# Fourier mixing and a token MLP on one core: both DFTs from a quarter of their matrices, with the symmetry compared on the chip

## The chip, the cores and the metric

The kernel runs on one core of a Trainium2 chip. A core has TensorE (PE) for matmuls, VectorE (DVE), ScalarE (ACT) and GpSimd (POOL) for elementwise work, SyncE (SP) which here issues most loads, and 16 DMA engines between DRAM and the core's memory (SBUF). Matmuls write into eight banks of PSUM. The engines run their own instruction streams in order and wait for each other through semaphores. The metric is the device time of one execution in microseconds; the time before is the median of three runs.

## The reference

One array `x` of 2048 rows (tokens) and 640 columns (channels) goes through a layer norm, and three terms are added:

```python
xn = _layernorm(x, axis=-1)
a = jnp.einsum("bsd,ed->bse", xn, dft_hid_re)
b = jnp.einsum("bsd,ed->bse", xn, dft_hid_im)
y = einsum("ts,bse->bte", dft_seq_re, a) - einsum("ts,bse->bte", dft_seq_im, b)
h = _layernorm(xn, axis=-1)
u = _gelu(jnp.einsum("bsd,sf->bdf", h, w1) + b1)
m = (jnp.einsum("bdf,fs->bds", u, w2) + b2).transpose(0, 2, 1)
return x + y + m
```

The DFT matrices are inputs like any other: two of 2048 x 2048 for the sequence and two of 640 x 640 for the hidden axis, cosines and sines, all float32. `w1` is 2048 x 1728 and `w2` 1728 x 2048; the host lays both out with the last half block repeated, as 14 blocks of 128.

## The kernel before, in words

Every float32 product is made of three passes of a faster matmul format, in `three` (L158): each operand is split into a high part, written by ACT (`high`, L149), and a low part, the rest, written by DVE (`low`, L152). A pass each for high times high, high times low and low times high goes into the same bank. So each matrix piece that comes from DRAM costs an ACT and a DVE instruction before PE can use it; `cut_piece` (L182) makes the two.

The work is a list of `steps`; a step cuts one piece and runs its products. `turn_of(i)` (L1236) writes out the instruction order by hand for step i: its loads, reads of finished banks and sums, then the high part of step i+2 (`AHEAD = 2`), extra work, waiting `jobs`, the low part of step i+2, and last the products of step i. Three tiles take turns for the cut pieces.

The stages run one after the other:

- `first_columns` (L505 and on) computes the first of four column blocks of the sequence DFT directly while rows of `x` still come in and are normalized. Its order is the string `START`.
- `columns` (L599 and on) does the other blocks with a seven-product scheme: of a 2 x 2 block product, seven products instead of eight, with sums of operands made by DVE. Each step is one 128 x 512 piece of the sequence matrices. Results go through `store_y` (L499) to DRAM, partly by accumulating DMA issued on GpSimd.
- `hidden` (L1048 and on) reads them back and multiplies by the hidden matrices, again with seven products, and `collect` (L1044) adds the result to `out` by an accumulating DMA. `out` was first filled with `x` by a copy inside DRAM.
- `up` (twice) and `down` (twice) are the MLP, 49 and 56 steps each, in `row_steps`, with seven products too. Their 128 x 512 or 128 x 384 weight pieces are loaded on SP four to six steps ahead into eight slots (`raw_slot`). Rows of `x` are loaded and normalized again for the MLP by `rows_again`, with the combined factors of the two layer norms from `factors_again`; `moving_of` makes their seven operands in six jobs.

Of the kernel before, what the change touches and what calls it, by code (L numbers as in the profile page):

```python
# [10 lines left out]
BF16 = mybir.dt.bfloat16  # L11
AF = mybir.ActivationFunctionType
ALU = mybir.AluOpType

P = 128
S = 2048
# [17 lines left out]
BLOCK = 10  # L34
APART = 2
FIRST_STEP = 6
LAST_ROWS = (3, 6, 7)


FIRST = [  # L40
    (0, 0, 0, 5), (1, 0, 0, 3), (0, 1, 0, 5), (1, 1, 0, 3), (0, 4, 0, 5), (0, 5, 0, 5), (1, 4, 0, 5), (1, 5, 0, 5),
    (1, 0, 3, 5), (1, 1, 3, 5),
]

FIRST_AT = [0, 6, 1, 7, 2, 3, 4, 5, 6, 7]

START = """
    x0 W0 b0 b1 x1 b2 x4 b3 x5 b4 x2 x3 b5 x6 x7 b6 b7  # L50
    M0 A0 R0 T0-0 T0-1 E0 D0-0-2 D0-2-5 T1 y0 B0 z0 n0 L0 B1 T2 M1 A1 E1 R1 O1 D1-0-2 H1-2-5 y1 B2 z1 P0-0 P0-1 P1-0 P0-2 P1-1 P1-2 M4-0 n1 L1-0-2 L1-2-5 M4-1
    A4 E4 T3 T4 R4 B3 O4 V4 H4 M5 A5 E5 R5 N4 O5 V5 B4 P2
    L4 P3 H5 T5 M2 A2 N5 M3 A3 R2-3 B5 F2-3 L5 q4 P4
    H2 T6 N2 M6 A6 B6 L2 q5 P5 T7 M7 B7 A7
"""

def jobs_at(ahead, behind=(), light=()):
    return tuple({i: at.count(i) for i in at} for at in (ahead, behind, light))  # L60


JOBS_AT = (
    jobs_at((0, 1, 2, 4, 10, 12, 13, 14, 15, 16, 17, 18, 23, 25, 27), (2, 4, 10, 15, 16, 16, 17, 17)),
    jobs_at((0, 1, 2, 3, 4, 10, 12, 13, 14, 15, 18, 19, 20, 21, 22, 23, 26, 27), (0, 1, 2, 3)),
    jobs_at((0, 1, 2, 3, 4, 5, 41), (0, 1, 2, 3)),
    jobs_at((0, 1, 2, 3, 4, 13, 18, 19, 22, 27), (), (10, 14, 21)),
)
# [3 lines left out]
    (tuple(i for i in range(56) if i % 7 in (0, 1, 3, 6) and i != 6), 56), ((0, 1, 3, 4), 7),  # L72
# [5 lines left out]
def fnet_plus_mixer(  # L78
# [20 lines left out]

# [20 lines left out]
    idea = keep.tile([P, 1], F32, name="idea")  # L120

    mv = keep.tile([P, NS, 2], F32, name="mv")
    norm = keep.tile([P, 2, NS], F32, name="norm")
    again = keep.tile([P, 2, NS], F32, name="again")
    near = keep.tile([P, 2, NS], F32, name="near")
# [5 lines left out]
    x_slab = [  # L131
        keep.tile([P, 7, D], F32, name="x0", tag="slab4"), keep.tile([P, 1, D], F32, name="x1", tag="slab5"),
    ]
    x_in = [x_slab[k // 7][:, k % 7, :] for k in range(8)]
    nc.gpsimd.memset(x_in[0][:, H2 : H2 + P], 0.0)
    nc.scalar.dma_start(x_in[0][:, H2:], x_rows[0][:, H2:])
    part_up = [dram.tile([P, 2, D], F32, name=f"up{r}") for r in range(NF2)]
    y_part = [[dram.tile([P, ND, CH], F32, name=f"y{m}{c}") for c in range(NC)] for m in range(2)]


    nc.gpsimd.memset(eps, EPS)
    nc.gpsimd.tensor_scalar(idea, eps, EPS, eps, op0=ALU.add, op1=ALU.mult)
# [23 lines left out]
    bank_turn = [3]  # L166
# [4 lines left out]

# [6 lines left out]

    def cut_piece(source, n, tail=False, stacked=False):  # L182


# [7 lines left out]
        def top(part=None):  # L192
            if part:
                hi = held["piece"][:, 0, : n // 2]
                high(hi, source()[:, : n // 2])
                nc.tensor.matmul(psum[7][: P // 4, : P // 4], hi[:, : P // 4], hi[:, : P // 4], start=True, stop=True)  # L196
                return
            cut_turn[0] = (cut_turn[0] + 1) % (AHEAD + 1)
            held["piece"] = keep.tile([P, 2, D], R32, name="piece", tag=f"cut{cut_turn[0]}")
            if tail:  # L200
                hi, _, src = of_tail()
                high(hi, src)
            elif part is None:
                high(held["piece"][:, 0, :n], source())
            else:
                nc.vector.tensor_copy(held["piece"][:, 0, n // 2 : n], source()[:, n // 2 :])
# [15 lines left out]


    stats = {}

    def statistics(k, row, *halves):
        if k not in stats:
            stats[k] = small.tile([P, 2, 6], F32, name="st")
        for i in halves or range(2):
            nc.vector.bn_stats(stats[k][:, i, :], row[:, i * H2 : (i + 1) * H2])  # L230

    def aggregate(k):
        nc.vector.bn_aggr(mv[:, k, :], stats[k].rearrange("p a b -> p (a b)"))

    def root(var, q=None):

        if q is None:
            q = small.tile([P, NS], F32, name="q")[:, : var.shape[-1]]
        nc.scalar.activation(q, var, AF.Abs_reciprocal_sqrt, bias=eps)
        return var, q  # L240
# [8 lines left out]
    def offset_beside(to, k):  # L249
        nc.gpsimd.tensor_scalar(to[:, 1, k : k + 1], mv[:, k, 0:1], to[:, 0, k : k + 1], -1.0, op0=ALU.mult, op1=ALU.mult)  # L250

    halves_of = {}

    def half_beside(k, engine=nc.gpsimd):
        halves_of[k] = small.tile([P, 1], F32, name="half")
        engine.tensor_scalar(halves_of[k], mv[:, k, 1:2], EPS, -0.5, op0=ALU.add, op1=ALU.mult)

    squares_of = {}

    def squares_beside(k, engine):  # L260
        r, q = small.tile([P, 1], F32, name="beside"), near[:, 0, k : k + 1]
        squares_of[k] = r
        engine.tensor_scalar(r, halves_of[k], q, q, op0=ALU.mult, op1=ALU.mult)

    def refined(k, engine):
        q = near[:, 0, k : k + 1]
        engine.tensor_scalar(norm[:, 0, k : k + 1], squares_of[k], 1.5, q, op0=ALU.add, op1=ALU.mult)

    def factors_beside(k):
        squares_beside(k, nc.gpsimd)  # L270
        refined(k, nc.gpsimd)
        offset_beside(norm, k)

    def offset(to, ks):
        nc.vector.scalar_tensor_tensor(to[:, 1, ks], mv[:, ks, 0], -1.0, to[:, 0, ks], op0=ALU.mult, op1=ALU.mult)

    def factors(ks):
        inverse(norm[:, 0, ks], *root(mv[:, ks, 1]))
        offset(norm, ks)

    def factors_again():

        f = []

        def rooted():
            var = small.tile([P, NS], F32, name="var2")
            nc.vector.tensor_mul(var, mv[:, :, 1], norm[:, 0, :])
            nc.vector.tensor_mul(var, var, norm[:, 0, :])
            f.append(root(var))

        def inverted():
            inverse(again[:, 0, :], *f[0])
            nc.vector.tensor_mul(again[:, 0, :], again[:, 0, :], norm[:, 0, :])
            offset(again, slice(0, NS))

        return [rooted, inverted]

    def normalize(k, row, by, to=None):
        nc.scalar.activation(
            row if to is None else to, row, AF.Identity, scale=by[:, 0, k : k + 1], bias=by[:, 1, k : k + 1]  # L300
        )
# [19 lines left out]

    Q = 256
    slot = {1: 0, 2: 1, 4: 2, 5: 3, 6: 4, 3: 5, 7: 6}
    at_slot = {0: 0, 6: Q, 1: D, 2: D + Q, 3: 2 * D, 4: 2 * D + Q, 5: 2 * D + 2 * Q}
    at_fifth = (2 * Q, D + 2 * Q)
    fixed = [[None] * 4 for _ in range(2)]

    def part(a, which, i, n=1):
        return a[:, which, at_slot[i] : at_slot[i] + n * Q]

    def fifth(a, which, i):
        return a[:, which, at_fifth[i] : at_fifth[i] + P]

    def place_fixed(h, q):
        fixed[h][q] = keep.tile([P, 2, 8 * Q], R32, name=f"n{h}{q}", tag=f"slab{4 * h + q}")

    def sums_of_rows(h, q, row, lower, apart=False):  # L340


        def a(of, i):
            return of()[:, i * Q : (i + 1) * Q]

        def hi(i, src):
            high(part(fixed[h][q], 0, i), src)

        def lo(i, src):
            low(part(fixed[h][q], 1, i), src, part(fixed[h][q], 0, i))  # L350

        def job1():
            nc.vector.tensor_add(a(lower, 1), a(row, 1), a(lower, 1))
            hi(3, a(lower, 1))

        def job2():
            lo(3, a(lower, 1))
            sub(a(lower, 1), a(lower, 1), a(row, 0))
            hi(4, a(lower, 1))

        def job3():
            lo(4, a(lower, 1))
            sub(a(lower, 0), a(lower, 0), a(lower, 1))
            hi(5, a(lower, 0))

        def job4():
            lo(5, a(lower, 0))
            sub(a(row, 1), a(row, 0), a(row, 1))
            if not apart:
                job5()  # L370

        def job5():
            hi(6, a(row, 1))

        def job6():
            lo(6, a(row, 1))

        return [job1, job2, job3, job4] + [job5] * apart + [job6]


    for q in range(4):
        place_fixed(0, q)

    def first_rows(k, which, *ends):

# [3 lines left out]
        if APART <= k < 4:  # L389
            ends = (0, 2, 4, 5)  # L390
# [925 lines left out]
```

## Time and profile before

| what | us |
|---|---|
| median of 3 runs | 866.54 |
| lowest and highest run | 865.94, 866.86 |
| span of the profiled execution, first to last instruction | 864.1 |
| PE busy in it | 860.2 |
| DVE busy | 695.3 |
| ACT busy | 522.7 |
| GpSimd busy | 158.0 |

The span lies 2.4 us under the median; that is what lies around the first and the last instruction. Busy time counts instructions from start to end as the profiler gives them; matmuls overlap their neighbours, so the duration of one is longer than the distance from one to the next. The granted TensorE clock is 1.000 throughout. DMA moved 154.44 MB.

### The profile page before, as it was taken

To read this page: it belongs to the slowest core of one execution; us is meant where nothing else is said; L and a number is where in the kernel's file an instruction comes from. 1 tells how busy PE (TensorE), PEld (TensorE's weight loads), DVE (VectorE), ACT (ScalarE), POOL (GpSimd) and SP (SyncE) were. 2 spreads that over 40 slices of the span, in tenths; PEclk is the share of its full clock that TensorE was granted. 3 is DMA by queue.
4 is the path that set the end of the run, shared out by engine and by line. 5 is a ranking of instruction groups with operands and counts; after the bars stand their busy time and mean duration, and the time that the engine had idled before them with its cause. 6 is when DMAs were issued, how large, how long until landed. Compare 5 with 4: busy or idle time off the path is not lost.

```text
span 864.1 us, 13905 instructions
## 1 busy us (share of the span) xinstructions
PE 860.2 (100%) x4900; PEld 789.5 (91%) x4900; DVE 695.3 (80%) x1176; ACT 522.7 (60%) x967; POOL 158.0 (18%) x215
## 2 busy tenths in 40 slices
PE   9999999999999999999999999999999999999998
PEld 7888888888888888889999999999999999999998
DVE  7898778758668888677877788888679978887887
ACT  5865575763555555447565556676667866555654
POOL 2222131210020211122100101111312221101211
PEclk9999999999999999999999999999999999999999
DMA  9949596795382746869576756665587789766776
GB/s 339 367 106 275 174 261 220 165 299 145 98 186 30 197 100 139 209 117 191 127 165 165 156 141 192 189 180 158 143 182 183 167 221 238 183 140 128 157 168 149
DMA packets 90293, 154.44 MB, mean 179 GB/s; under 512 B 9008, under 2 KB 37424, under 8 KB 89968
## 3 DMA queue, kind: packets, MB, share of 16 engines
q0 software_dynamic: 25008, 57.52, 35.8%
q1 hardware_dynamic: 64928, 95.80, 33.7%
q8 instruction: 38, 0.62, 0.3%
q10 hardware_dynamic: 288, 0.25, 0.1%
q14 instruction: 31, 0.25, 0.1%
HBM read 99.96 MB, written 58.82 MB: 184 GB/s over the span
## 4 chain that ended last, share of the span: by engine, by line
PE 100%; DVE 0%; DVEq 0%; issue 0%
PE psum L161 32%; PE psum L162 32%; PE psum L164 31%; PE psum L526 3%; PE psum L147 0%; DVE pair L966 0%; DVEq L1312 0%; PE psum L196 0%
## 5 line engine op out<-in xcount | busy, mean ns | idle before, releaser
L153 DVE TENSOR_TENSOR piece<-pieces,piece 128x512 fp32r<-128x512 f32 (+4 forms) x496 | 326.9, 659 | 128.7 <-ACT piece L150 125.6
L150 ACT ACTIVATE piece<-pieces 128x512 fp32r<-128x512 f32 (+3 forms) x472 | 295.1, 625 | 220.6 <-PE psum L164 138.8
L161 PE MATMUL psum<-piece,n 128*128 128x512 f32 x540 | 210.1, 389 | 0.0
L162 PE MATMUL psum<-piece,n 128*128 128x512 f32 x540 | 210.1, 389 | 0.0
L164 PE MATMUL psum<-piece,n 128*128 128x512 f32 x540 | 210.1, 389 | 0.0
L162 PE MATMUL psum<-sup,piece 128*128 128x320 f32 x392 | 120.8, 309 | 0.0
L161 PE MATMUL psum<-sup,piece 128*128 128x320 f32 x392 | 120.8, 309 | 0.0
L162 PE MATMUL psum<-sdown,piece 128*128 128x320 f32 x392 | 120.8, 309 | 0.0
L161 PE MATMUL psum<-sdown,piece 128*128 128x320 f32 x392 | 120.8, 309 | 0.0
L161 PEld LDWEIGHTS psum<-piece,n 128*128 128x128 f32 x540 | 101.4, 188 | 21.2
L164 PEld LDWEIGHTS psum<-piece,n 128*128 128x128 f32 x540 | 101.4, 188 | 20.9
L162 PEld LDWEIGHTS psum<-piece,n 128*128 128x128 f32 x540 | 101.4, 188 | 20.9
L156 DVE TENSOR_TENSOR pieces<-pieces 128x512 f32<-128x512 f32 (+3 forms) x142 | 111.8, 792 | 3.0
L164 PE MATMUL psum<-sup,piece 128*128 128x320 f32 x368 | 113.7, 309 | 0.0
L164 PE MATMUL psum<-sdown,piece 128*128 128x320 f32 x368 | 113.7, 309 | 0.0
L503 POOL DMA_DIRECT2D y<-c x65 | 56.0, 898 | 255.3 <-DVE c L703 153.9
L164 PE MATMUL psum<-shid,piece 128*128 128x320 f32 x280 | 86.5, 309 | 0.0
L162 PE MATMUL psum<-shid,piece 128*128 128x320 f32 x280 | 86.5, 309 | 0.0
L161 PE MATMUL psum<-shid,piece 128*128 128x320 f32 x280 | 86.5, 309 | 0.0
L161 PEld LDWEIGHTS psum<-sdown,piece 128*128 128x128 f32 x392 | 73.6, 188 | 0.0
L161 PEld LDWEIGHTS psum<-sup,piece 128*128 128x128 f32 x392 | 73.6, 188 | 0.0
L162 PEld LDWEIGHTS psum<-sup,piece 128*128 128x128 f32 x392 | 73.6, 188 | 0.0
(136 smaller groups left out, 1105.9 us busy)
## 6 DMA issues: line engine op xcount, KB each, us to landing
pieces<-in_dft_seq SPq DMA_DIRECT2D x120, 256.0 KB, 5.3
y<-c POOLq DMA_DIRECT2D x105, 256.0 KB, 5.1
pieces<-in_w SPq DMA_DIRECT2D x88, 256.0 KB, 3.7
out<-pair POOLq DMA_DIRECT2D x36, 320.0 KB, 5.3
pieces<-y SPq DMA_DIRECT2D x32, 320.0 KB, 4.0
pieces<-in_w SPq DMA_DIRECT2D x32, 192.0 KB, 2.6
out<-in_x SPq DMA_DIRECT2D x16, 320.0 KB, 8.0
up<-pair POOLq DMA_DIRECT2D x8, 640.0 KB, 3.2
```

What stands on the lines that cost most here:

```text
L150: nc.scalar.activation(hi, src, AF.Copy)
L153: nc.vector.tensor_sub(lo, src, hi.bitcast(F32))
L156: nc.vector.tensor_sub(to, a, b)
L161: nc.tensor.matmul(psum, wh, mh, start=first, stop=False, skip_group_check=True)
L162: nc.tensor.matmul(psum, wh, ml, start=False, stop=last and wl is None, skip_group_check=True)
L164: nc.tensor.matmul(psum, wl, mh, start=False, stop=last, skip_group_check=True)
L503: nc.gpsimd.dma_start(y_part[m][c][:, j, :], t, accum_op=ALU.add)
L526: nc.tensor.matmul(banks[m, j], channels(k, j)[rows], w[cols], start=n == 0 and k == begin, stop=n == 2 and k == end, skip_group_check=True,)
```

## The change

The Fourier part is written anew; the MLP stages keep their code, apart from where their operands lie in SBUF.

- Rows are loaded in four groups of 512: rows p x 2 + r of a block j in the upper and lower half of `x`, four rows on each partition. All four are normalized (`moments`, `rooted`, `factors`, `normalized`). DVE adds row s and row s + 1024 (`row_sums`), and GpSimd subtracts them (`row_differences`): the sums are what even output rows need, the differences the odd ones.
- `folded` adds and subtracts column d and column 640 - d, read backwards, and sorts by the parity of d. DVE does this for the sums, GpSimd for the differences. `f_high` and `f_low` split the result.
- The sequence DFT is four rounds, one for each of the matrices `m` and each parity of the output row (`seq_round`). A round is 8 steps of 9 matmuls, in six banks. A step cuts every second column of two 128-row blocks of the upper left quarter of the matrix. The sums and differences of the two row parities give output rows t and t + 1024; they stay in SBUF as `t_all`.
- The hidden DFT is 16 steps of 18 matmuls of 320 columns (`hid_step`); a sum and a difference give columns e and e + 320. The result goes to `out` by accumulating DMA as before. The trip of intermediate results through DRAM is gone.
- The factors of the second normalization are written to DRAM and read back in row order (`again_factors`).
- 32 `seq_unit`s and 6 `hid_unit`s load every entry of the four matrices, combine it with its partner, and sum the squares of what is left into a column of `off`. A unit has two places in turn in `slab4`. Its load is on SP at step i, its compare on GpSimd at step i+3, its square on ACT at step i+4. The hidden units begin at steps 34, 37 and on, nine sequence units at steps 52, 55 and on, in the first `up`, and 23 from two steps into the first `down`, 4.5 steps apart. The second `up` has none.
- `scale_check` looks at the first row, and `verdict`, three steps before the end, makes one number `bad`: 1 where a sum of squares is above 2^-64. If it is 1, `in_general` computes everything again from the full matrices.

```diff
+    def row_sums(j):
+        nc.vector.tensor_add(rows(j, 2), rows(j, 0), rows(j, 1))
+
+    def row_differences(j):
+        nc.gpsimd.tensor_sub(rows(j, 0), rows(j, 0), rows(j, 1))
...
+    def folded(j, odd, engine, tag):
...
+        for begin, n, at, at_b in ((0, Q, 0, H2), (Q, 64, Q, H2 + Q)):
+            ahead, back = z[:, :, begin : begin + n], z[:, :, D - begin : D - begin - n : -1]
+            engine.tensor_add(to(at, n), parted(ahead), parted(back))
+            engine.tensor_sub(to(at_b, n), parted(ahead), parted(back))
+        engine.tensor_copy(ft[:, :, H2 : H2 + 1], z[:, :, H2 : H2 + 1])
+
+    def f_high(j, odd):
+        high(f_part(odd, j, 0), folds[j, odd])
+
+    def f_low(j, odd):
+        low(f_part(odd, j, 1), folds[j, odd], f_part(odd, j, 0))
...
+    rounds = ((1, 0), (1, 1), (0, 0), (0, 1))
+    windows = ((0, P, 2 * P), (H2, H2 + P, 4 * P))
+
+    def seq_round(n, m, odd):
...
+                def products(w, j=j, r=r):
+                    for i, at in enumerate(windows[m]):
+                        if j == 0:
+                            banks[r, i] = bank()
+                        f = [f_part(odd, j, which)[:, r, at : at + P] for which in range(2)]
+                        three(banks[r, i], f, [a[:, :CH] for a in w], j == 0, j == NJ - 1)
...
+            for near, far, b in of:
+                nc.vector.tensor_add(near, far, b)
+                nc.vector.tensor_sub(far, far, b)
...
+    def hid_step(n, h, odd, i):
...
+            for blocks in (((T0, 0), (T2, 2), (T3, 4)), ((T1, 1), (T2, 3), (T4, 5))):
+                b = bank()
+                banks.append(b)
+                for e, (block, of) in enumerate(blocks):
+                    three(
+                        b[:, :H2], [a[:, block * P : (block + 1) * P] for a in w],
+                        [hid_m[0][:, which, of, :] for which in range(2)], e == 0, e == 2,
+                    )
...
+            nc.scalar.activation(odd_part, banks[1][:, :H2], AF.Copy)
+            nc.vector.tensor_add(y[:, :H2], banks[0][:, :H2], odd_part)
+            nc.vector.tensor_sub(y[:, H2:], banks[0][:, :H2], odd_part)
+            nc.gpsimd.dma_start(out_pairs[h, i, odd], y, accum_op=ALU.add)
...
+    def seq_unit(u, place):
...
+            for i, (h, col) in enumerate(((0, c), (1, c), (0, c + 2), (1, c + 2))):
+                nc.sync.dma_start(t[:, i, :], seq_rows[NC * m + col, h, j, :, r])
...
+            eng = nc.gpsimd
+            (eng.tensor_add if r else eng.tensor_sub)(t[:, 2:4, :], t[:, 0:2, :], t[:, 2:4, :])
+            a, b = (t[:, i, :].rearrange("p (q v) -> p v q", v=2) for i in range(2))
+            eng.tensor_sub(b[:, 0], a[:, 0], b[:, 0])
+            eng.tensor_add(b[:, 1], a[:, 1], b[:, 1])
...
+            v = t[:, 1:4, :]
+            nc.scalar.activation(v, v, AF.Square, accum_out=off[:, u : u + 1])
...
+            (nc.gpsimd.tensor_add if m else nc.gpsimd.tensor_sub)(back, base, back)
+            nc.vector.scalar_tensor_tensor(base[:, :H2], base[:, :H2], sign, base[:, H2:], op0=ALU.mult, op1=ALU.subtract)
...
+    for j in range(1, NJ):
+        i = 2 * (j - 1)
+        if j + 1 < NJ:
+            at(i, moments, j + 1, when=reads)
+            at(i, rooted, j + 1, when=reads)
+        at(i, row_sums, j, when=reads)
+        at(i, folded, j, 0, nc.vector, "ca", when=reads)
+        at(i, f_high, j, 0, when=reads)
+        if j + 1 < NJ:
+            at(i, factors, j + 1, when=reads)
+        at(i, row_differences, j, when=extras)
+        at(i, f_low, j, 0, when=behind_lo)
+    for j in range(NJ):
+        at(2 * j if j < 3 else 5, folded, j, 1, nc.gpsimd, "cb" if j < 3 else "ca", when=extras)
...
+    def unit_at(i, make, by=3):
+        u = []
+        loads[i].append(lambda: (u.extend(make()), u[0]()))
+        extras[i + by].append(lambda: u[1]())
+        extras[i + by + 1].append(lambda: u[2]())
...
+    with tc.If(nc.values_load(bad[0:1, 0:1], min_val=0, max_val=1) > 0):
+        in_general()
```

More of the change, by code (lines that the diff above doesn't have):

```diff
@@ L32 @@
 WARM = 15
[L34 to L68, printed above, removed]
+NJ = 4
+NR = 2
+Q = 256
+DZ = D + 2
+T3, T4, T2, T0, T1 = range(5)
+N_SEQ = 2 * 2 * NJ * NR
+N_HID = NS
+NEAR = 2.0**-64
+FAR = 0.5
 LONG_AT = (
-    (tuple(i for i in range(56) if i % 7 in (0, 1, 3, 6) and i != 6), 56), ((0, 1, 3, 4), 7),
+    (), ((0, 1, 3, 4), 7),
     (tuple(i for i in range(49) if i % 7 in (0, 1, 3, 6) and i not in (45, 48)), 49), ((0, 1, 3), 7),
@@ L190, in of_tail, with top @@
             return hi[:, :, :TAIL], hi[:, :, P - TAIL :], src[:, :, :TAIL]
[L192 to L199, printed above, removed]
+        def top():
+            held["piece"] = cut_tile()
             if tail:
@@ L221, in cut_piece, with cut_view, top, bottom @@
         return top, bottom
[L224 to L240, printed above, removed]
+    def cut_view(view, parts):
+        held = []
+        def top():
+            held.append(cut_tile())
+            high(view(held[0][:, 0]), parts())
+        def bottom():
+            low(view(held[0][:, 1]), parts(), view(held[0][:, 0]))
+            return held[0][:, 0], held[0][:, 1]
+        return top, bottom
     def inverse(to, var, q):
@@ L265, in refined @@
[L265 to L279, printed above, removed]
@@ L320, in fnet_plus_mixer @@
     }
[L325 to L378, printed above, removed]
@@ L742, in job0 @@
         def job0():
[L743 removed]
+            moving[stage, q] = home(stage, q)
             hi(0, piece(0, 0))
@@ new lines, in fnet_plus_mixer @@
+        x_load(0)
+        x_load(1)
+        w_load(1, 0)
+        x_load(2)
+        w_load(1, 1)
+        x_load(3)
+        w_load(1, 2)
+        w_load(1, 3)
+        for i in range(2, 4):
+            nc.gpsimd.memset(rows(i, 0).rearrange("p (r d) -> p r d", r=NR)[:, :, D:], 0.0)
+            nc.gpsimd.memset(rows(i, 1).rearrange("p (r d) -> p r d", r=NR)[:, :, D:], 0.0)
+        nc.scalar.activation(one, eps, AF.Abs_reciprocal_sqrt)
+        moments(0)
+        rooted(0)
+        factors(0)
```

809 lines of the change are left out of this document (414 added, 395 removed).

## The prediction

> **What bounds the kernel now.** I read the busy line and the chain first, then the stages, then the shapes.
>
> ```profile
> PE 860.2 (100%) x4900; PEld 789.5 (91%) x4900; DVE 695.3 (80%) x1176; ACT 522.7 (60%) x967; POOL 158.0 (18%) x215
> ...
> PE 100%; DVE 0%; DVEq 0%; issue 0%
> ```
>
> PE is never idle and the whole chain is PE, so time now equals the number of matmuls times their spacing. The table of stretches cuts the span where the matmuls change. Its columns are the stretch, its length, busy time (and instructions) of PE, PEld, DVE, ACT and POOL, then the granted clock, the DMA share and GB/s.
>
> ```profile
> 5.10:32.50 27.40, 27.40 (x123) 22.56 (x122) 25.34 (x68) 17.66 (x35) 6.55 (x14) 1.00 1.02 375
> 32.50:399.70 367.20, 367.20 (x1622) 304.15 (x1621) 282.78 (x439) 215.21 (x386) 73.36 (x98) 1.00 0.68 176
> 399.70:522.90 123.20, 123.20 (x842) 123.20 (x841) 100.02 (x144) 68.71 (x114) 14.54 (x17) 1.00 0.68 161
> 522.90:607.30 84.40, 84.40 (x578) 84.40 (x577) 71.05 (x120) 57.88 (x110) 9.29 (x13) 1.00 0.60 177
> 607.30:691.90 84.60, 84.60 (x579) 84.59 (x578) 69.52 (x117) 61.37 (x121) 22.61 (x27) 1.00 0.74 168
> 691.90:790.40 98.50, 98.50 (x673) 98.50 (x673) 83.27 (x142) 58.99 (x107) 17.66 (x23) 1.00 0.76 185
> 790.40:860.80 70.40, 70.40 (x482) 70.32 (x480) 60.94 (x144) 40.75 (x92) 13.07 (x16) 1.00 0.73 158
> ```
>
> These are, in order, the first columns, the rest of the sequence DFT, the hidden DFT, up0, up1, down0 and down1.
>
> ```profile
> L161 PE MATMUL psum<-piece,n 128*128 128x512 f32 x540 | 210.1, 389 | 0.0
> ...
> L161 PE MATMUL psum<-sup,piece 128*128 128x320 f32 x392 | 120.8, 309 | 0.0
> ...
> L161 PE MATMUL psum<-shid,piece 128*128 128x320 f32 x280 | 86.5, 309 | 0.0
> ```
>
> The durations of 389 and 309 ns overlap; the spacing counts. Three passes of 540 in 367.2 us are 0.2267 us for a 512-wide matmul; three passes of 280 in 123.2 us are 0.1467 us for a 320-wide one. The four MLP stretches take 337.9 us and keep all their matmuls. DVE is busy 84%, 85% and 87% of up0, down0 and down1: little room for more.
>
> **The change, part by part.** *Matmuls.* The Fourier part falls from 27.4 + 367.2 + 123.2 = 517.8 us to 32 steps of 9 matmuls of 512 columns (288 x 0.2267 = 65.3 us, 16.3 for each of four rounds) and 16 steps of 18 of 320 columns (288 x 0.1467 = 42.2 us). If PE stayed the bound, some 410 us would go. It will not stay the bound; the rest is about what comes late instead.
>
> *Vector prices.*
>
> ```profile
> L153 DVE TENSOR_TENSOR piece<-pieces,piece 128x512 fp32r<-128x512 f32 x354 | 243.6, 688 | 105.3 <-ACT piece L150 103.3
> L153 DVE TENSOR_TENSOR piece<-pieces,piece 128x640 fp32r<-128x640 f32 x56 | 45.9, 822 | 15.3 <-ACT piece L150 15.1
> L156 DVE TENSOR_TENSOR pieces<-pieces 128x512 f32<-128x512 f32 x66 | 45.2, 685 | 1.2
> L961 DVE TENSOR_TENSOR pair<-psum,pair 128x320 f32<-128x320 f32 x75 | 36.5, 486 | 7.5 <-PE psum L164 7.2
> L156 DVE TENSOR_TENSOR pieces<-pieces 128x1024 f32<-128x1024 f32 x28 | 34.1, 1219 | 0.0
> ...
> L230 DVE BATCH_NORM_STATS2 st<-x 128x6 f32<-128x320 f32 x16 | 7.2, 480 | 3.0 <-DMA x<-in_x 3.0
> ```
>
> From 512 to 1024 elements a DVE instruction grows by 0.53 us, so about 1.04 ns an element plus 0.16 us. One group of 512 rows (four rows a partition) then costs DVE: statistics 4 x (2 x 0.48 + an aggregate, taken as half of one) = 4.8; row sum of 1284 elements 1.5; column fold, two of 512 and two of 128 elements and a copy, 2.1; low part of 1280 elements 1.5.
>
> ```profile
> L150 ACT ACTIVATE piece<-pieces 128x512 fp32r<-128x512 f32 x353 | 221.8, 629 | 164.3 <-PE psum L164 112.5 <-DVE piece L153 15.7 <-DVE c L703 7.0
> ...
> L299 ACT ACTIVATE pair<-pair,again 128x640 f32<-128x640 f32 x12 | 10.9, 912 | 0.0
> ```
>
> On ACT: four normalizations 3.65 us, a high part of 1280 elements at the 512-wide row's rate 1.5.
>
> *GpSimd arithmetic*, which no row shows: the row difference, the odd fold and the compares. The nearest rows only write:
>
> ```profile
> L1080 POOL MEMSET pair<- 64x640 f32 x1 | 0.6, 627 | 3.8 <-DMA pair<-up 3.8
> ...
> L135 POOL MEMSET x<- 128x128 f32 x1 | 0.2, 205 | 0.3 <-POOLq L1305 0.3
> ```
>
> That is 0.82 ns an element and 0.1 us fixed. Reading two operands and writing one is bounded by one such pass (0.82) and three in sequence (2.46). I take two, 1.64, because two operands must be read: row difference 2.2 us, fold 2.6, compare of a sequence unit (1024 + 256 + 256 elements) 2.8. The Trainium skill, "GPSIMD Engine Reference", 3.1, measures 4497 ns for a two-input add of 2048 elements, 2.2 ns each; by it the same sum as below would come to about 619 us.
>
> *Do GpSimd and DVE run side by side?* In the opening GpSimd runs one-element instructions:
>
> ```profile
> 14.91 0.27 POOL L267 TENSOR_SCALAR norm<-beside,near 128x1 f32<-128x1 f32 x1
> ...
> 15.91 0.85 POOL L263 TENSOR_SCALAR beside<-half,near 128x1 f32<-128x1 f32 x1
> 16.86 0.70 POOL L267 TENSOR_SCALAR norm<-beside,near 128x1 f32<-128x1 f32 x1
> ```
>
> ```profile
> 14.29 0.88 DVE L230 BATCH_NORM_STATS2 st<-x 128x6 f32<-128x320 f32 x2
> ...
> 15.86 0.69 DVE L153 TENSOR_TENSOR piece<-pieces,piece 128x512 fp32r<-128x512 f32 x1
> 16.59 0.84 DVE L153 TENSOR_TENSOR n<-x,n 128x640 fp32r<-128x640 f32 x1
> ```
>
> Beside a statistics instruction L267 takes 0.27 us. Beside a DVE subtraction of two SBUF tiles it takes 0.70 and ends at 17.56, just after DVE's 17.43; L263 takes 0.85 and ends at 16.76, after DVE's 16.55. A tiny GpSimd instruction waited out DVE's two-operand instruction. That direction is shown; that DVE in turn waits out a long GpSimd one is not, since none is long. I bound the loss between nothing and the whole GpSimd duration, and take the whole for DVE's two-operand share, as exclusion works both ways. The Trainium skill, "SBUF — State Buffer", "Who interferes with whom", says that a DVE instruction with two SBUF inputs contends with a GpSimd instruction that reads SBUF and the later one fully blocks; the rows agree in the direction they show.
>
> *Opening and round 0.*
>
> ```profile
> x<-in_x SPq DMA_DIRECT2D x1, 160.0 KB, 2.3
> ...
> b_sb<-in_b SPq DMA_DIRECT2D x1, 7.0 KB, 2.8
> ```
>
> 160 KB land 2.3 us after issue; issued near 0.8, two loads of 640 KB at 375 GB/s (first stretch) land at about 4.4 and 6.2. Statistics of group 0 end at 9.2; root and factors (small) 10.3; statistics of group 1, which stand ahead on DVE, 15.1; row sum 16.6; fold 2.1 with the row difference of 2.2 in its way 20.9; high part 22.4; cuts and low part 25.9. The first product comes at about 24, against 5.1 now. Then each further group is a loop on DVE and ACT: 4.8 + 1.5 + 2.1 + GpSimd 2.2 + high 1.5 + cut 0.63 + 0.69 + low 1.5 + GpSimd's odd fold 2.3 + second cut 0.69 = 17.9. Group 1 ends at 43.8, group 2 (with an odd low part) at 63.2, group 3 (no statistics, an odd low part) at 77.8. PE needs 4.1 us per group. Round 0 ends at **80**.
>
> *Rounds 1 to 3.* DVE needs 8 cuts, 6 combinations and two low parts, 12.6 us of 16.3. PE bounds; 2 us are added per change of banks: 3 x 18.3 = 55, to **135**. The matrix loads (1 MB each), the factors' trip through DRAM and the setting up of the checks lie under this.
>
> *Hidden DFT.* DVE: 16 x (0.82 + 0.49 + 0.49) = 28.8; three of up0's four operands at 4.75 (7 instructions) 14.3; last combinations 4.1; hidden checks 2.9; first sums of up0 2.1; GpSimd in the way 5 x 1.15 = 5.8. That is **58** against PE's 42.2, to 193.
>
> *MLP and checks.* Each unit loads 1 MB, GpSimd compares 2.8 us, ACT squares 1536 elements (1.9 us). Of DVE's time some 87% is two-operand work (the rest reads PSUM), so a unit takes 2.45 us from DVE. Nine in up0, three steps apart: 5.28 us there hold 4.45 of DVE; 4.45 + 2.45 - 5.28 = 1.62 late, 14.6 in all. Twelve in down0, 4.5 steps or 7.92 us apart: 6.69 + 2.45 - 7.92 = 1.22, 14.7. Eleven in down1, 5.66 apart: 4.90 + 2.45 - 5.66 = 1.69, 18.6. Together **48**; 83 at 2.46 ns an element, nothing without exclusion. The MLP ends at 193 + 338 + 48 = 579.
>
> Three waits are new. GpSimd's compare waits for its load; behind it stand GpSimd's accumulating stores. ACT's square waits for GpSimd; behind it stand the next high parts. SP's check load waits for the square two units back; behind it stand the weight loads. Two steps cut ahead, 3.5 us, cover the second; three steps between load and compare the first. ACT's squares (3.62 + 1.9 = 5.5 us in up0's 5.28) hide under the late DVE; without it they cost 2 us.
>
> *DMA.* 1.05 MB at 375 GB/s is 2.85 us of share one. In up0 0.60 x 5.28 + 2.85 = 6.0; down0 8.9 of 7.92; down1 7.0 of 5.66: 6.6 + 11.4 + 14.5 = 32 us late alone. DVE is later, so it hides this.
>
> *End.* The last matmul to the end of span stays 3.3 us (864.1 - 860.8). Loading the verdict and branching over the general path on every engine has no row; nothing to a small load's 2.8 us, doubled. I take 3.
>
> Sum: 579 + 3.3 + 3 = 585 of span. The profiled span is 864.1, the median 866.54; the 2.4 outside it stay: **588 us**.
>
> **Rivals.** *GpSimd doesn't hold DVE*: round 0 ends at 64, hidden 52, and the MLP is stretched by DMA alone: 64 + 55 + 52 + 370 + 8.7 = 550. For it: no row shows DVE held. *DMA has slack too*: 518; against it, share times length above. *In-order waits pile up*: loads behind 1 MB checks and squares behind compares cost more than two steps cover, a further 50 us: 640. For it: the DMA sums over one. *The general path runs*: one pair off by more than 2^-32 on one partition decides it. It would come after everything: 640 wide and 1216 narrow matmuls (640 x 0.2267 + 320 x 0.1467 + 896 x 0.1467) are 323 us at this trace's spacing at least, so 911 or more, slower than before. Against it: as the reference computes these matrices, partners differ by at most 1.5e-12.
>
> **How the numbers follow.** Forecast 588, 0.58 (between 560 and 634 by GpSimd's price). 550: 0.2. 518 or less: 0.1. 640 or more: 0.09. General path: 0.03. The range 518 to 634 leaves about 2 in 10 out. A measurement tells 0.2% from no change; all but the last lie far below: faster 0.97, same 0, slower 0.03.
>
> **What would show it.** First product near 24 us; PE in bursts of two steps until 80; DVE nearly full until 193; long DVE subtractions beside GpSimd's compares and PE gaps of 1 to 2 us per unit in up0 and the down stages, none in up1. Wrong if DVE's mean durations stay 688 there, if PE waits for DMA, or if instructions follow the verdict.

## The result, and the profile after

The changed kernel takes **682.28 us** (median of four runs, 678.72 to 685.22) against 866.35 for the kernel before in the same session: a ratio of 0.787, 95% interval 0.785 to 0.790. It is faster by 184 us. The prediction was 588 us, with a range of 518 to 634, so the direction was right and the time lies 94 us beyond the forecast and 48 us beyond the upper end.

The profiled execution took 678.72 us with a span of 676.9. First its busy lines and the clock that PE was granted in 40 equal slices:

```profile
PE 510.3 (75%) x2896; PEld 468.8 (69%) x2896; DVE 517.9 (77%) x786; ACT 359.7 (53%) x645; POOL 275.5 (41%) x241
...
PEclk7666779898989798678999999979978898989997
```

PE was busy for 100% of the span before and is now busy for 75%. No engine is full on average, and the clock is below 0.9 in two thirds of the slices in which PE had gaps (20 of 30). The table of stretches cuts the span where the matmuls change; the columns are those of the table in the prediction. In order: up to the first product, round 0 (with the first six matmuls of round 1), rounds 1 to 3, hidden DFT, up0, up1, down0, down1.

```profile
0.00:22.40 22.40, 4.00 (x16) 1.55 (x16) 14.92 (x39) 7.32 (x11) 3.77 (x14) 0.67 0.91 345
22.40:78.90 56.50, 30.75 (x78) 20.75 (x78) 46.27 (x65) 21.49 (x28) 25.61 (x19) 0.68 0.13 49
78.90:141.20 62.30, 55.05 (x212) 42.64 (x212) 41.51 (x70) 33.77 (x52) 4.67 (x8) 0.89 0.54 170
141.20:194.40 53.20, 45.07 (x289) 43.76 (x288) 40.70 (x70) 29.32 (x53) 24.77 (x23) 0.97 0.87 185
194.40:333.60 139.20, 98.68 (x582) 95.72 (x581) 91.00 (x140) 75.31 (x138) 55.31 (x45) 0.87 0.64 194
333.60:417.20 83.60, 83.60 (x572) 83.60 (x572) 68.54 (x116) 61.30 (x121) 22.83 (x27) 1.00 0.74 167
417.20:559.20 142.00, 110.17 (x676) 105.62 (x676) 117.30 (x141) 74.53 (x131) 76.18 (x58) 0.92 0.82 226
559.20:670.70 111.50, 83.04 (x483) 75.12 (x481) 97.08 (x149) 56.69 (x116) 62.34 (x49) 0.95 0.77 195
```

The MLP starts at 194.4, where the forecast had 193. The whole miss lies behind that point, and only in the three stages that carry comparing units. up1, which has none, takes 83.6 us with PE full, as before. up0, down0 and down1 take 139.2, 142.0 and 111.5 where the prediction had 99, 113 and 89.

Two views show what GpSimd does there. First DVE's low part of a weight piece in the groups by shape, then the tile of the units on GpSimd (shortest, median and longest duration in ns):

```profile
L121 DVE TENSOR_TENSOR piece<-xa,piece 128x512 fp32r<-128x512 f32 x160 | 135.2, 848 | 72.1 <-ACT piece L118 71.9
```

```profile
L478 POOL TENSOR_TENSOR checks<-checks x32: 2347/2692/3359, 226.7 to 653.4; 128x1024 f32<-128x1024 f32 x32
L480 POOL TENSOR_TENSOR checks<-checks x32: 833/1050/1412, 229.5 to 656.1; 128x256 f32<-128x256 f32 x32
L481 POOL TENSOR_TENSOR checks<-checks x32: 835/1226/1442, 230.3 to 656.9; 128x256 f32<-128x256 f32 x32
```

The same DVE operation took 688 ns before and takes 848 on average now. The shortest durations of a unit's three compares add up to 2.35 + 0.83 + 0.84 = 4.0 us; the prediction had 2.8. The opening shows what happens when the two meet, in the timeline (start, duration, instruction):

```profile
16.62 0.69 DVE L302 TENSOR_TENSOR ft<-big 128x512 f32<-128x512 f32 x1
17.22 2.98 DVE L301 TENSOR_TENSOR ft<-big 128x128 f32<-128x128 f32 x1
20.12 0.28 DVE L302 TENSOR_TENSOR ft<-big 128x128 f32<-128x128 f32 x1
```

```profile
17.00 3.06 POOL L269 TENSOR_TENSOR big<-big 128x1284 f32<-128x1284 f32 x1
```

An addition of 128 elements on DVE takes 2.98 us while GpSimd's row difference runs from 17.00 to 20.06, and its twin right behind it takes 0.28. This is the direction that the trace of before could not show: DVE waits out a long GpSimd instruction.

Third, a stall in up0 that no long instruction explains:

```profile
226.15 0.92 POOL L911 DMA_DIRECT2D up<-pairs  x1 [7.30 <-DMA up<-pair]
226.74 2.70 POOL L478 TENSOR_TENSOR checks<-checks 128x1024 f32<-128x1024 f32 x1
...
230.31 0.83 POOL L481 TENSOR_TENSOR checks<-checks 128x256 f32<-128x256 f32 x1
...
231.18 1.48 ACT L485 ACTIVATE checks<-checks 128x1536 f32<-128x1536 f32 x1 [11.13 <-POOL checks L481]
...
233.61 0.62 ACT L118 ACTIVATE piece<-xa 128x512 fp32r<-128x512 f32 x1
234.13 0.42 ACT L805 ACTIVATE pair<-psum 128x320 f32<-128x320 f32 x1
...
234.26 0.69 DVE L121 TENSOR_TENSOR piece<-xa,piece 128x512 fp32r<-128x512 f32 x1 [11.11 <-ACT piece L118]
...
234.60 0.63 PE L129 MATMUL psum<-sup,piece 128*128 128x320 f32 x1 [10.27 <-ACT pair L805]
```

The brackets give how long the engine had been idle and who released it. An accumulating store on GpSimd waited 7.3 us for an earlier store to land. The compare stood behind it, ACT's square waited 11.1 us for the compare, the high part of the next weight piece stood behind the square, and DVE's low part behind the high part. PE was idle for 10.3 us; what released it last was ACT's read of a finished bank (L805), which stood behind the square as well. Every wait but the first follows from instruction streams that run in order.

Such waits add up. Two lines of the profile's page give the first compare of a unit and the square, with the idle time before them:

```profile
L478 POOL TENSOR_TENSOR checks<-checks 128x1024 f32<-128x1024 f32 x32 | 85.6, 2675 | 35.9 <-DMA checks<-in_dft_seq 34.1
L485 ACT ACTIVATE checks<-checks 128x1536 f32<-128x1536 f32 x32 | 47.3, 1479 | 65.1 <-POOL checks L481 59.1
```

GpSimd waited 34.1 us for the units' loads to land, and ACT 59.1 us for compares.

### The profile page after: what moved, and what is told of

Its sections match the earlier page's. It is cut to its first block, busy times and chain, and to the rows that moved or that the text cites. A ratio compares the mean times of both kernels' runs of the same rounds, so it can differ in the third digit from the quotient of the medians.

```text
span 676.9 us, 8855 instructions
## 1 busy us (share of the span) xinstructions
PE 510.3 (75%) x2896; PEld 468.8 (69%) x2896; DVE 517.9 (77%) x786; ACT 359.7 (53%) x645; POOL 275.5 (41%) x241
## 4 chain that ended last, share of the span: by engine, by line
## 5 line engine op out<-in xcount | busy, mean ns | idle before, releaser
L121 DVE TENSOR_TENSOR piece<-xa,piece 128x512 fp32r<-128x512 f32 (+3 forms) x246 | 199.5, 813 | 81.2 <-ACT piece L118 79.5
L118 ACT ACTIVATE piece<-xa 128x512 fp32r<-128x512 f32 (+2 forms) x222 | 131.1, 595 | 79.4 <-PE psum L132 35.6
L129 PE MATMUL psum<-sup,piece 128*128 128x320 f32 x245 | 81.1, 332 | 33.2 <-ACT pair L805 27.5
L132 PE MATMUL psum<-big_moving,piece 128*128 128x320 f32 x282 | 90.9, 323 | 19.9 <-DVE piece L121 19.4
L129 PE MATMUL psum<-big_moving,piece 128*128 128x320 f32 x315 | 99.7, 317 | 6.2 <-ACT pair L805 4.5
L478 POOL TENSOR_TENSOR checks<-checks 128x1024 f32<-128x1024 f32 x32 | 85.6, 2675 | 35.9 <-DMA checks<-in_dft_seq 34.1
L130 PE MATMUL psum<-big_moving,piece 128*128 128x320 f32 x315 | 98.6, 314 | 0.0
L129 PE MATMUL psum<-sdown,piece 128*128 128x320 f32 x224 | 73.1, 326 | 21.7 <-ACT pairs L803 10.8
L485 ACT ACTIVATE checks<-checks 128x1536 f32<-128x1536 f32 x32 | 47.3, 1479 | 65.1 <-POOL checks L481 59.1
L132 PE MATMUL psum<-sup,piece 128*128 128x320 f32 x230 | 76.1, 331 | 7.3 <-DVE piece L121 7.3
L132 PE MATMUL psum<-sdown,piece 128*128 128x320 f32 x224 | 73.3, 327 | 10.1 <-DVE piece L121 10.1
L130 PE MATMUL psum<-sup,piece 128*128 128x320 f32 x245 | 79.9, 327 | 0.0
L129 PEld LDWEIGHTS psum<-sup,piece 128*128 128x128 f32 x245 | 50.3, 205 | 35.0 <-ACT pair L805 28.9
L132 PEld LDWEIGHTS psum<-big_moving,piece 128*128 128x128 f32 x282 | 54.6, 194 | 25.0 <-DVE piece L121 25.0
L130 PE MATMUL psum<-sdown,piece 128*128 128x320 f32 x224 | 71.9, 321 | 0.0
L124 DVE TENSOR_TENSOR xa<-xa 128x512 f32<-128x512 f32 (+1 forms) x90 | 67.3, 755 | 2.2
L129 PEld LDWEIGHTS psum<-big_moving,piece 128*128 128x128 f32 x315 | 60.9, 193 | 8.5 <-ACT pair L805 5.5
L130 PEld LDWEIGHTS psum<-big_moving,piece 128*128 128x128 f32 x315 | 60.9, 193 | 0.0
L132 PEld LDWEIGHTS psum<-sdown,piece 128*128 128x128 f32 x224 | 44.5, 199 | 12.5 <-DVE piece L121 12.3
```

The costliest lines, as they stand in the source:

```text
L118: nc.scalar.activation(hi, src, AF.Copy)
L121: nc.vector.tensor_sub(lo, src, hi.bitcast(F32))
L124: nc.vector.tensor_sub(to, a, b)
L129: nc.tensor.matmul(psum, wh, mh, start=first, stop=False, skip_group_check=True)
L130: nc.tensor.matmul(psum, wh, ml, start=False, stop=last and wl is None, skip_group_check=True)
L132: nc.tensor.matmul(psum, wl, mh, start=False, stop=last, skip_group_check=True)
```

## The experiments

Two theories stood against each other. **Exclusion**: GpSimd's compare and DVE's two-operand work on SBUF run one after the other, so a unit costs DVE most of GpSimd's duration, which was priced too low. **Waits in order**: the units' loads, compares and squares hold up what stands behind them on SP, GpSimd and ACT, whatever DVE does. DMA share was a third suspect. A kernel whose time is given without an interval was executed once. The four executions of the changed kernel spread over 6.5 us, and those of the all-DVE kernel below over 11.1 us, so a difference of less than some 11 us between totals of single executions is not read as an effect.

**No units, and loads alone.** The first kernel leaves out loads, compares and squares; the second keeps the loads. Wherever squares are left out, the sums in `off` are set to zero.

```diff
-        loads[i].append(lambda: (u.extend(make()), u[0]()))
-        extras[i + by].append(lambda: u[1]())
-        extras[i + by + 1].append(lambda: u[2]())
+        return
```

> All 38 check units are left out (loads, compares, squares; the sums are set to zero). The changed kernel spends 139, 84, 142 and 112 us in up0, up1, down0 and down1, where the matmuls alone need 338 in all. If the units are the whole loss there, the four stages come back to about 338 us and the total to about 682 - 138 = 544 us. If the matmuls' half clock or the new places of the operands cost something of their own, the stages stay above 350.

```diff
         loads[i].append(lambda: (u.extend(make()), u[0]()))
-        extras[i + by].append(lambda: u[1]())
-        extras[i + by + 1].append(lambda: u[2]())
```

> Only the loads of the units remain (no compares, no squares). Theory M (the 1 MB loads fill the DMA engines and the weights come late): the MLP is at least 32 us over 338, total 575 or more. Theories W (in-order waits: a GpSimd store that waits, the compare behind it, ACT's square behind that, the high parts behind the square) and X (GpSimd's compare and DVE's two-operand work exclude each other): within 5 us of the kernel without units, about 545.

Measured: 535.59 and 553.35 us. Without units, up0, down0 and down1 (in this order) look like this:

```profile
184.10:272.50 88.40, 85.83 (x581) 84.91 (x581) 76.91 (x133) 58.90 (x113) 10.21 (x14) 1.00 0.63 178
...
355.80:454.50 98.70, 98.70 (x675) 98.70 (x675) 83.51 (x142) 59.40 (x108) 17.62 (x24) 1.00 0.76 186
454.50:527.90 73.40, 71.40 (x487) 70.96 (x485) 62.15 (x149) 40.67 (x92) 13.82 (x16) 1.00 0.72 153
```

The prediction charged the units with 48 us in the MLP and, in the hidden DFT, with 2.9 us of DVE's own work and 5.8 us for GpSimd in its way: 56.7 in all. Without them it is 588 - 56.7 = 531.3, so everything but the units was forecast 4 us too low in sum. The units cost 682.3 - 535.6 = 146.7 us, 90 more than forecast, and that is nearly the whole miss of 94. Loads alone:

```profile
190.60:279.30 88.70, 85.78 (x580) 84.86 (x580) 77.34 (x133) 59.39 (x114) 11.37 (x15) 1.00 0.88 289
...
362.80:466.40 103.60, 99.97 (x675) 98.82 (x675) 83.38 (x143) 59.04 (x108) 17.77 (x24) 1.00 1.02 307
466.40:544.20 77.80, 73.13 (x485) 72.24 (x483) 62.17 (x148) 40.47 (x92) 13.54 (x16) 0.98 0.99 280
```

The DMA share goes to 1.02 and 0.99 in the down stages, which are 4 to 5 us longer each. DMA is full there, but 17.8 us in the whole kernel is not the bulk of 147.

**Compares without squares, and later squares.** The first kernel leaves out the squares; the second runs them one step later in up0 and four steps later in the down stages.

```diff
-        extras[i + by + 1].append(lambda: u[2]())
```

> Loads and compares remain, ACT's squares are left out, so nothing on ACT, DVE or PE waits for GpSimd's compares any more, while they still take their time beside DVE. Theory W: most of the 138 us goes, total 560 to 600. Theory X: DVE still loses about the whole GpSimd time, total 640 or more. DVE's 512-wide low part stays near 848 ns under both.

```diff
-        extras[i + by + 1].append(lambda: u[2]())
+        extras[i + by + after].append(lambda: u[2]())
```

Here `after` is 2 for the hidden units and in up0, and 5 in the down stages.

> Everything is computed, but ACT's square stands one step later in up0 and four steps later in the down stages than before, so the compare has more time before ACT waits for it. Theory W: 30 to 80 us faster, 600 to 650, most of it in down0 and down1. Theory X: no more than 10 us faster.

Measured: 655.03 and 665.06 us. So compares cost 655.0 - 553.4 = 101.7 us over the loads and squares 27.3 more. The first total is what exclusion expected. Moving the squares later gains 17.2 us, between what the two theories expected, and this is a net gain: SP's check loads now wait 63.5 us for squares to free their slots, where they waited 12.3. Waits behind ACT's square are real and the smaller part. Without squares, DVE fills up0, down0 and down1:

```profile
196.00:320.30 124.30, 98.49 (x581) 94.58 (x580) 108.76 (x139) 60.45 (x114) 59.22 (x44) 0.90 0.71 217
...
404.00:537.20 133.20, 110.53 (x675) 106.32 (x674) 126.65 (x142) 59.81 (x108) 79.37 (x59) 0.94 0.85 241
537.20:645.30 108.10, 86.96 (x483) 81.48 (x483) 99.75 (x148) 41.15 (x92) 61.82 (x49) 0.87 0.78 200
```

DVE's busy time grew over the kernel without units by 108.76 - 76.91 = 31.85 us in up0, 43.14 in down0 and 37.60 in down1, while its count of instructions changed by at most 6 in a stage. For 9, 12 and 11 units that is 3.5, 3.6 and 3.4 us a unit (in up0 an upper value, since two of the hidden units' compares fall there too), the prediction's 87% of 4.0 us.

**GpSimd only writes.** The compares are replaced by five clearings of 1024 elements (three of 640 for a hidden unit), about as long, which read nothing. Squares are left out, so this stands beside the kernel without squares.

```diff
-            eng = nc.gpsimd
...
-            eng.tensor_sub(b[:, 0], a[:, 0], b[:, 0])
-            eng.tensor_add(b[:, 1], a[:, 1], b[:, 1])
+            for _ in range(5):
+                nc.gpsimd.memset(t[:, 2:4, :], 0.0)
```

> As c_no_square (loads and GpSimd work, no squares), but each compare is replaced by five memsets of 1024 elements (three of 640 in a hidden unit): GpSimd is about as long busy, and reads no SBUF. The comparison is left out. Theory X: DVE isn't held, the total falls from 655 to about the 553 of loads alone, DVE's 512-wide low part back at about 688 ns. Theory Q: GpSimd's queue is as full as before, so the total stays above 630.

Measured: 585.61 us, 69.4 less than with compares. The kernel without squares had been expected to keep DVE's low part near the changed kernel's 848 ns; it rose to 948. This low part, first in the kernel without squares and then in this one (L122 is the same line in both):

```profile
L122 DVE TENSOR_TENSOR piece<-xa,piece 128x512 fp32r<-128x512 f32 x160 | 151.3, 948 | 33.8 <-ACT piece L119 33.6
```

```profile
L122 DVE TENSOR_TENSOR piece<-xa,piece 128x512 fp32r<-128x512 f32 x160 | 110.1, 688 | 51.8 <-ACT piece L119 50.6 <-PE psum L133 1.0
```

```profile
186.40:298.70 112.30, 93.85 (x581) 91.35 (x580) 81.97 (x140) 59.88 (x114) 60.66 (x70) 0.89 0.78 244
...
382.60:486.20 103.60, 100.59 (x676) 100.33 (x675) 83.42 (x142) 59.09 (x107) 69.48 (x77) 0.98 0.99 297
486.20:576.50 90.30, 79.11 (x482) 77.75 (x481) 62.78 (x148) 41.10 (x92) 71.09 (x76) 0.91 0.90 250
```

GpSimd is as busy in up0 (60.66 us against 59.22), 12% less in down0 and 15% more in down1, yet DVE's mean is back at 688 ns, and down0 is back at the 103.6 of loads alone. It is not a busy GpSimd that holds DVE but one that reads. The Trainium skill, "SBUF — State Buffer", "Who interferes with whom", states it so: a DVE instruction with two SBUF inputs contends with a GpSimd instruction that reads SBUF, not with one that only writes. 948 against 688 ns agrees.

What remains over the loads alone is 32.3 us, most of it in up0 (112.3 against 88.7) and down1 (90.3 against 77.8). The waits of this kernel in up0 (total, number, longest) name a place:

```profile
SPq L475 <- POOL checks L479: 32.6, 7, 9.4
```

SP's next check load waited seven times, 32.6 us in all, for GpSimd to be done with the slot, and the weight loads stand behind it on SP. In the same stretch ACT waited 17.8 us for weight pieces to land.

**The compares on DVE.** If DVE must wait for GpSimd anyway, its own compare should be cheaper.

```diff
-            eng = nc.gpsimd
+            eng = nc.vector
...
-            (nc.gpsimd.tensor_add if m else nc.gpsimd.tensor_sub)(back, base, back)
+            (nc.vector.tensor_add if m else nc.vector.tensor_sub)(back, base, back)
```

> The compares run on DVE, in their old places, instead of GpSimd; squares and loads as in the changed kernel. Theory X (GpSimd's compare and DVE's two-operand work exclude each other, and GpSimd needs 4.0 us where DVE needs about 2.1): DVE's 512-wide low part falls from 848 to about 688 ns, a unit takes about 2.1 us of DVE instead of 3.5, total 600 to 635. Theory Q (GpSimd is merely busy, and its stores come late behind the compares): DVE's low part stays at 848 ns. If DVE stands waiting for a unit's loads in its turn, the total may come out near 680 all the same.

Measured: 610.56 us, 71.7 less than the changed kernel.

```profile
L121 DVE TENSOR_TENSOR piece<-xa,piece 128x512 fp32r<-128x512 f32 x160 | 109.5, 687 | 31.4 <-ACT piece L118 31.2
...
L478 DVE TENSOR_TENSOR checks<-checks 128x1024 f32<-128x1024 f32 x32 | 39.1, 1221 | 11.6 <-DMA checks<-in_dft_seq 11.6
L480 DVE TENSOR_TENSOR checks<-checks 128x256 f32<-128x256 f32 x32 | 13.6, 426 | 1.1
L481 DVE TENSOR_TENSOR checks<-checks 128x256 f32<-128x256 f32 x32 | 13.4, 420 | 0.0
```

The low part is back at 687 ns. A unit's compare takes DVE 1.22 + 0.43 + 0.42 = 2.07 us of its own in place of the 3.5 that it lost to GpSimd. For 32 units that is 46 us, and the hidden DFT is 7.7 us shorter (45.5 against 53.2); the other 18 of the 71.7 us were not separated. Up0, down0 and down1 still take 110.5, 119.6 and 100.1 us, 70 more than without units, and these were not taken apart either.

The same with the later squares was expected to gain further:

> As e_compare_dve, with the squares later too: one step in up0, four in the down stages. Theory X with the waits of ACT behind the compare as a second, smaller part (17 us by d_square_later): 5 to 20 us faster than e_compare_dve, 585 to 620.

Measured: 625.12 us, 14.6 slower instead of faster. Most of it lies in down1 (111.6 us against 100.1). SP's waits in the two down stages, first with later squares, then without:

```profile
SPq L474 <- ACT checks L485: 58.7, 16, 7.2
```

```profile
SPq L474 <- ACT checks L485: 4.0, 2, 2.0
```

A unit has two slots. A later square frees its slot later, so the load two units on waits at the head of SP's stream, with the weights behind it. That the delay which helps ACT's stream hurts SP's is read from these waits; no run varies the number of slots.

**The opening on DVE.** Row differences and odd folds go to DVE; the folds of groups 1 and 2 move one step later, behind the low parts.

```diff
-        nc.gpsimd.tensor_sub(rows(j, 0), rows(j, 0), rows(j, 1))
+        nc.vector.tensor_sub(rows(j, 0), rows(j, 0), rows(j, 1))
...
-    for j in range(NJ):
-        at(2 * j if j < 3 else 5, folded, j, 1, nc.gpsimd, "cb" if j < 3 else "ca", when=extras)
+    for j in (0, 3):
+        at(2 * j if j < 3 else 5, folded, j, 1, nc.vector, "cb" if j < 3 else "ca", when=extras)
...
+        if j < 2:
+            at(i + 1, folded, j + 1, 1, nc.vector, "cb", when=behind_lo)
```

> Only the opening is changed: the row differences (1284 elements) and the column folds of the differences run on DVE, not GpSimd. Theory X: DVE takes 3.6 us a group itself, where it lost 4.5 or more to GpSimd; round 0 ends 3 to 12 us before the changed kernel's 78.8 us, the total falls by as much. If GpSimd ran beside DVE for free, the opening would be 12 us longer.

Measured: 666.63 us, 15.6 less, somewhat more than expected. Round 0's 72 matmuls end at 65.1 us instead of 77.6, and the first product of the hidden DFT comes at 125.3 instead of 141.2. In the opening's timeline the difference now costs DVE 1.49 us, and the 128-element addition is short again:

```profile
17.25 0.29 DVE L301 TENSOR_TENSOR ft<-big 128x128 f32<-128x128 f32 x1
...
18.38 1.49 DVE L269 TENSOR_TENSOR big<-big 128x1284 f32<-128x1284 f32 x1
```

**Everything on DVE.** This kernel joins the last two edits, with the squares where the change has them.

> Both moves at once: the compares (as e_compare_dve) and the opening's differences and folds (as h_opening_dve) on DVE. Theory X: the two savings (72 and 16 us) touch different stages and add up: 590 to 600.

Measured: **592.17 us** (587.31 to 598.42, four runs), a ratio of 0.682 to the kernel before (0.679 to 0.685). The two savings add up as expected. With the next variant, which can't be told from it, this is the best version found, 90 us under the changed kernel, and it computes all that the change computes. Three variants followed. The first spreads the units more evenly: six in up0, and one every four steps from the first down on.

> As i_all_dve, with six units in up0 instead of nine and 26 units from the first down on, 4 steps apart instead of 4.5. A unit costs up0 about 2.4 us (110 against 89 us of the loads alone, nine units) and the down stages about 1.7: 0 to 5 us faster than i_all_dve.

Measured: 591.46 us, ratio 0.685 (0.681 to 0.688): no difference that can be told. The other two issue the units' loads on GpSimd, to take them out of SP's stream: one from the all-DVE kernel, one from the kernel in which GpSimd only writes.

```diff
-                nc.sync.dma_start(t[:, i, :], seq_rows[NC * m + col, h, j, :, r])
+                nc.gpsimd.dma_start(t[:, i, :], seq_rows[NC * m + col, h, j, :, r])
```

> As i_all_dve, with the sequence units' loads issued on GpSimd instead of SP, so no weight load on SP stands behind a check load that waits for its place. If that order costs time once DVE compares, 5 to 25 us faster than i_all_dve; SP waited little for squares there (4 us in the down stages), so it may also change nothing, or be slower by GpSimd's 0.9 us for each issue.

> As g_writes_only (memsets on GpSimd in place of the compares, no squares), with the sequence units' loads issued on GpSimd. In g_writes_only SP waited 32.6 us for GpSimd in up0 with the weight loads queued behind, and up0 took 112 us against 88.5 with loads alone. If that wait is up0's loss, up0 returns to 95 or less and the total to 555 to 570; if it is GpSimd's late stores, up0 stays above 105.

Measured: 621.27 us, ratio 0.715 (0.712 to 0.719), slower than with the loads on SP; and 708.23, against 585.61 with the loads on SP. In the second, up0 takes 122.6 us, where 95 or less was expected if SP's order was the loss and more than 105 if it was GpSimd's late stores. Neither kernel shows what SP's order alone costs, because the move loads GpSimd instead, as the waits of the second show:

```profile
POOL checks L479 <- DMA checks<-in_dft_seq: 92.2, 23, 7.3
...
ACT pair L804 <- DMA out<-pair: 64.9, 6, 19.4
```

```profile
L475 POOL DMA_DIRECT2D checks<-in_dft_seq x128: 546/548/1251, 201.5 to 685.1; - x128
```

Issuing one of these loads takes GpSimd at least 0.55 us, four to a unit. Its clearings wait 92.2 us for loads (28.8 with the loads on SP), and ACT waits 64.9 us for accumulating stores to free their source tiles (10.7 with the loads on SP). The queue with the waits moved to the engine that issues the stores. So what the 32.3 us of a merely busy GpSimd consist of stays open. That a different split of loads among queues gains something is not excluded; it wasn't tried.

## Why the prediction was right and wrong

**Opening and sequence DFT: right in time.** First product at 22.4 us (forecast 24), round 0 done at 77.6 (80), in bursts. GpSimd holds DVE, as assumed: 2.98 against 0.28 us for one addition. But GpSimd's prices were too low here too: the row difference takes 3.06 us, not 2.2, and the four additions and subtractions of an odd fold 3.9 us (78.2 to 82.1, beside a DVE that is idle until 81.9), where 2.6 were taken for the whole fold. That the time came out right all the same is luck: another term was too high, and which one was not found. Rounds 1 to 3 take 62.3 us, not 55: ACT had just waited 6.5 us for GpSimd's odd fold of group 2, and the first 16 us run at a granted clock of 0.68.

**Hidden DFT: right by two errors.** It ends at 194.4 (193), but takes 53.2 us where 58 were forecast, which offsets rounds 1 to 3. The forecast counted DVE as full there. DVE is busy for 40.7 of 53.2, part of up0's operands having been cut before, from 131.9 on. Without units it takes 44.1 us, so the hidden units cost 9.1, close to the forecast's 2.9 + 5.8 = 8.7.

**MLP: the step that failed.** "Together 48" became 139.2 + 83.6 + 142.0 + 111.5 - 338 = 138 us. It failed in two places, and the second is the larger:

- *"I take two, 1.64."* A 1024-element compare takes 2.35 us at the least, and the unit 4.0 instead of 2.8. The prediction's own formula with 0.875 x 4.0 = 3.5 us a unit gives 9 x 2.67 + 12 x 2.27 + 11 x 2.74 = 81 us instead of 48. The mechanism was right, DVE's growth of 3.4 to 3.6 us a unit confirms it, and only its size was off. This price lies inside the bracket that the prediction gave (83 us at 2.46 ns), so by itself it would have left the time within the range. The Trainium skill, "GPSIMD Engine Reference", 3.1, has 4497 ns for 2048 elements, 2.2 ns each, and that was the better figure: 2347 ns for 1024 elements are 2.29. The estimate of 619 us that the prediction worked out from it lies inside the range and still below the time.
- *"Two steps cut ahead, 3.5 us, cover the second; three steps between load and compare the first"*, and *"DVE is later, so it hides this"* of DMA. They do not cover them: GpSimd waits 34.1 us for loads, ACT 59.1 us for compares. The third wait, SP's, was named and given no price at all, and SP's check loads wait 37.8 us for compares and 12.3 us for squares. Not all of this reaches PE. Put together step by step, the runs give 17.8 of the 146.7 us to the loads, 32.3 to GpSimd being merely busy, 69.4 to its reading and 27.3 to the squares; the shares hold for this order of adding the parts. By the formula, price 81 and hidden 9 are 90, and the remainder is some 57 us. The forecast had nothing for it. It is about the 50 us of the rival "in-order waits pile up", which was put as an alternative at 0.09 and came on top of the forecast instead. But a remainder is no measurement: that in-order waits and a full DMA are in it is shown, how it divides is not.

A gap in PE also has an aftermath that no term held. PE's busy time in up0 is 98.68 us against 84.40 before, for 582 and 578 matmuls, at a granted clock of 0.87. Part of the wait is thus paid a second time as slow matmuls; how much this costs by itself was not separated. The gaps were not the forecast's "1 to 2 us per unit" either: the one shown is 10.3 us.

**End: right.** From the last matmul to the end of the span it is 676.9 - 670.7 = 6.2 us (6.3 forecast), and 1.8 us lie outside the span (2.4).

**Rivals.** "GpSimd doesn't hold DVE" fell: 948 against 688 ns. "DMA has slack too" held in up0, where loads alone cost 0.3 us, and fell in the down stages and the hidden DFT, where they cost 4 to 5 us each. The general path did not run: PE has 2896 matmuls, where that path would have added 1856.

**The range** took the price of GpSimd and the waits in order as cases of which one happens. They act together: the price alone gives 588 + 33 = 621, and the 50 us of waits on top give 671. An upper end so built would have come within 11 us of the time.

## What to carry to other kernels

Arithmetic given to GpSimd beside a DVE that is full of two-operand SBUF work is not off the path: charge its whole duration, times DVE's share of such work, to DVE, and compare that with DVE's own price (here 3.5 against 2.1 us a unit). Work that is added at intervals to in-order streams needs each stream walked on its own: the slot's release at the head of the load queue, the store ahead of the compare, the square ahead of the cut; a delay that frees one can block another. When two costs can act on the same stretch, the range must hold their sum, not the larger.

## What was not expected of the hardware

GpSimd's two-operand addition or subtraction takes 2347 ns for 1024 elements and 833 ns for 256 with every second element taken, at the least: 1.97 ns an element and a fixed 0.33 us if the stride costs nothing. DVE takes 1221 and 426 ns on average for the same shapes.

After an idle stretch PE runs slower for some time. In the timeline of the changed kernel's round 0, PE after a gap of 9.3 us:

```profile
39.77 0.80 PE L129 MATMUL psum<-piece,f 128*128 128x512 f32 x1 [9.30 <-ACT piece L118]
...
44.62 0.63 PE L132 MATMUL psum<-piece,f 128*128 128x512 f32 x1
45.05 0.47 PE L129 MATMUL psum<-piece,f 128*128 128x512 f32 x1
45.36 0.40 PE L130 MATMUL psum<-piece,f 128*128 128x512 f32 x1
45.60 0.40 PE L132 MATMUL psum<-piece,f 128*128 128x512 f32 x1
```

From 42.49 to 45.05 the starts lie 0.43 us apart, and 0.24 behind 45.36: nearly twice the distance until more than 5 us after the gap, with one short wait of 0.61 us in between. A stall on such a kernel costs more than its own length.
